# Sending the first four chunks' y to the partitions of their modes through TensorE instead of through transfers

## Chip, cores, metric

One core of a Trainium2 chip. The metric is the device time of one execution in microseconds, taken as the median of repeated runs; the spans in the profile run from the first to the last instruction and are some 2 us shorter.

## The reference, cut to what matters

```python
attn_out = softmax(causal(q @ k.T / 8) + min(bias(s), 0)) @ v        # per batch and head
x  = attn_out -> (8, 576, 512)
X  = rfft(x, axis=1)[:, :64]                                         # 64 modes
Yr = einsum('bmd,mde->bme', Xr, w_r) - einsum('bmd,mde->bme', Xi, w_i)
Yi = einsum('bmd,mde->bme', Xr, w_i) + einsum('bmd,mde->bme', Xi, w_r)
y  = irfft(Y, n=576, axis=1)
u  = x + y
out = u + relu(u @ w_ch)
```

The 64 modes have two weight matrices of 512x512 in fp32 each: 134 MB that pass through the core once. Modes are worked in eight chunks of eight. `y` in the kernel is a chunk's (Yr, Yi) before the inverse transform. Its rows lie on partitions as (mode part, batch); the inverse transform needs a tile `yv` whose partitions are the mode parts alone, with batch in the free dimension, for both `y` and `y @ w_ch`.

## The kernel before

```python
def spread(c, which, rows):                    # one transfer of 128 KB inside SBUF
    nc.sync.dma_start(out=yv[16 * c : 16 * c + 16, :, which, :], in_=rows)

def modes(g, c, meanwhile=None):               # four loads of 512 KB, four column groups
    ps = auxpool.tile([P, DM], FP32, name="yp", tag="aux")
    ...                                        # 16 matmuls; L441
    else:                                      # the last group of channels
        yb = spool.tile([P, DM], FP16, name="y_sb", tag="y")
        ...                                    # yb = ps + y_acc; L455
        spread(c, 0, yb)
        return yb

def first_times_wch(b):                        # y @ w_ch of chunks 0 to 3, one batch; L644, L648
    vp = auxpool.tile([P, DM], FP32, name="v_ps", tag="aux")
    n = 2 * MC * NY                            # 64
    for dt in range(DT):
        nc.tensor.matmul(
            vp[:n], yt_first[:, dt].rearrange("p c (x b) -> p (c x) b", b=B)[:, :, b],
            wch_sb[:, dt, :], start=(dt == 0), stop=(dt == DT - 1),
        )
    nc.vector.tensor_copy(out=yv[:n, b, 1, :], in_=vp[:n])

TAKE = (3, 2, 2, 0, 2, 1)                      # pieces of the x work after each chunk
for c in range(NCK - 2):
    yb = modes(NG - 1, c)
    for x in range(TAKE[c] - 1):
        work()
    yt = y_transposed(yb, c)                   # kept in yt_first for c < NY = 4
    if TAKE[c]:
        work()
    if c >= NY:
        y_times_wch(c, yt)                     # product, copy, spread(c, 1, vb)
    elif c == NY - 1:
        for b in range(B):
            first_times_wch(b)
work()
...                                            # chunks 6 and 7, then 32 output tiles
```

`auxpool` has two PSUM tiles of 128x512 fp32; `upool` has two of 128x512 and `zpool` two of 128x1024. (The expectations call a piece of 128x512 a bank.) So `y @ w_ch` of the first four chunks already goes through kept transposes (a batch's 64 columns are the stationary operand; the trace has weight loads of 128x64 at L644 and copies of 64x512 from `v_ps` to `yv` at L648), while their `y` goes by transfer.

The softmax here doesn't subtract the row's maximum and nothing guards it: scores larger than these inputs give would overflow.

## Time and profile before

| | before |
|---|---|
| median of 3 runs (range) | 459.39 us (458.98 to 459.42) |
| span of the profiled run | 457.1 us |
| DMA engines full | in slices 1 to 36 of 40 |
| last weight load consumed | 418.11 us |
| tail after it | 39.0 us |
| gather after chunk 3, on TensorE | 377.18 to 386.13 us |

The first two rows are results; the others come from the views that the prediction quotes. The kernel is a stream of weight loads with a tail of 39.0 us that the change leaves as it is. In a timeline line the columns are start in us, length in us, engine, source line, operation, output and inputs, shapes and count; brackets give the idle time before it and what ended it. PE is TensorE's matmuls, PEld its weight loads, DVE VectorE, ACT ScalarE, POOL GpSimd, SP SyncE. The clock that is quoted is the share of its full clock that TensorE was granted. The gather is the stage after chunk 3 that brings results of chunks 0 to 3 to the partitions of `yv`; the tail is all that follows the last load; a closed run is a stretch of TensorE work without waits.

### The profile page before, as it was taken

How to read it: one execution, taken by the hardware profiler on the slowest of the kernel's cores; microseconds unless marked ns; L12 is line 12 of the kernel's file. 1: busy time of each engine (PE TensorE's matmuls, PEld its weight loads, DVE VectorE, ACT ScalarE, POOL GpSimd, SP SyncE). 2: the span in 40 equal slices, each digit the busy share in tenths (PEclk: the TensorE clock that was granted, in tenths of full speed). 3: DMA queues.
4: the chain of work that ended last, by engine and by line, in shares of the span. 5: the costliest groups of instructions: out<-in, count | busy, mean ns of one | idle time of the engine just before them, and what ended most of it. 6: DMA issues, size and time to landing. Idle time of an engine off the chain costs nothing.

```text
span 457.1 us, 10262 instructions
## 1 busy us (share of the span) xinstructions
PE 339.1 (74%) x4177; PEld 217.2 (48%) x4209; DVE 237.3 (52%) x528; ACT 219.1 (48%) x382; POOL 182.9 (40%) x269
## 2 busy tenths in 40 slices
PE   1779968966562979936587766779967769797995
PEld 1556646644341656614355544446643326343432
DVE  7777645653242556624345544466656425442675
ACT  1587856554241747723445345446622220221895
POOL 6755555544345555344454444355423223200000
PEclk9999999998586889957778799899999778999999
DMA  9999999999999999999999999999999999995688
GB/s 177 201 203 203 202 201 204 202 204 204 204 204 201 202 202 202 204 205 204 199 192 205 204 204 204 204 203 202 207 206 212 210 210 210 214 214 105 235 285 319
DMA packets 109375, 94.54 MB, mean 207 GB/s; under 512 B 28480, under 2 KB 104512, under 8 KB 109328
## 3 DMA queue, kind: packets, MB, share of 16 engines
q0 software_dynamic: 98960, 81.81, 113.0%
q1 hardware_dynamic: 10368, 12.07, 8.5%
q8 instruction: 33, 0.54, 0.4%
q14 instruction: 14, 0.11, 0.1%
HBM read 164.56 MB, written 9.44 MB: 381 GB/s over the span
## 4 chain that ended last, share of the span: by engine, by line
DMA 70%; PE 20%; issue 4%; POOL 3%; DVE 2%; DVEq 0%; POOLq 0%
DMA w_sb<-in_moe_w_i_dram 44%; DMA q<-in_q_dram 13%; DMA w_sb<-in_moe_w_r_dram 5%; PE yp L441 3%; PE sc_ps L365 3%; PE av_ps L394 2%; DMA x_all<-in_moe_w_r_dram 2%; DMA k<-in_k_dram 2%; PE sc_ps L359 2%; DMA y_acc<-in_moe_w_i_dram 2%; PE tr_ps L324 2%; DMA y_acc<-in_moe_w_r_dram 2%; PE u_ps L694 2%; PE z_ps L675 2%; PE u_ps L675 2%
## 5 line engine op out<-in xcount | busy, mean ns | idle before, releaser
L373 ACT ACTIVATE p_sb<-sc_ps,cumt_sb 128x576 f16<-128x576 f32 (+1 forms) x256 | 141.9, 636 | 45.8 <-PE sc_ps L365 45.4
L217 POOL DMA_DIRECT2D w_sb<-in_moe_w_i_dram x60 | 45.1, 751 | 81.7 <-PE yp L441 36.8
L217 POOL DMA_DIRECT2D w_sb<-in_moe_w_r_dram x60 | 45.4, 757 | 65.2 <-DMA w_sb<-in_moe_w_r_dram 26.1
L217 POOL DMA_DIRECT2D v<-in_v_dram x72 | 50.8, 707 | 31.3 <-DMA w_sb<-in_moe_w_r_dram 8.4
L324 PE MATMUL tr_ps<-ident,q 64*64 64x64 bf16 x576 | 17.1, 208 | 55.4 <-DMA q<-in_q_dram 55.4
L359 PE MATMUL sc_ps<-negm,ident 128*128 128x256 bf16 x256 | 55.0, 300 | 0.3
L441 PE MATMUL yp<-w_sb,xs 128*32 128x512 bf16 x480 | 37.0, 408 | 22.2 <-DMA w_sb<-in_moe_w_i_dram 18.1
L327 DVE COPY qtA<-tr_ps 64x576 bf16<-64x576 bf16 x32 | 23.8, 743 | 50.8 <-PE tr_ps L324 50.7
L344 ACT ACTIVATE p<-sc_ps,cumt 128x64 f16<-128x64 f32 x32 | 10.1, 314 | 74.2 <-PE sc_ps L340 74.2
L394 PE MATMUL av_ps<-v,p_sb 128*128 128x65 f16 x1024 | 43.7, 196 | 0.0
L394 PEld LDWEIGHTS <-p_sb 128*128 128x128 f16 x1024 | 38.9, 99 | 4.8 <-issue 0.7
L327 DVE COPY ktA<-tr_ps 64x576 bf16<-64x576 bf16 x32 | 24.0, 750 | 32.7 <-PE tr_ps L324 32.7
L324 PEld LDWEIGHTS <-q 64*64 64x64 bf16 x576 | 13.3, 120 | 58.0 <-DMA q<-in_q_dram 56.9
L441 PEld LDWEIGHTS <-xs 128*32 128x32 bf16 x512 | 22.9, 169 | 32.3 <-issue 28.8
L365 PE MATMUL sc_ps<-qtB,ktB 128*128 128x64 bf16 (+2 forms) x160 | 34.8, 322 | 3.7 <-issue 2.4
L365 PE MATMUL sc_ps<-qtA,ktA 65*128 65x512 bf16 (+2 forms) x192 | 36.1, 297 | 0.3 <-DVE ktA L327 0.3
L399 DVE TENSOR_REDUCE den<-av_ps 128x5 f32<-128x10 f32 x64 | 10.8, 169 | 46.4 <-PE av_ps L394 46.4
L404 DVE TENSOR_TENSOR x_all<-av_ps,rcp 128x320 f16<-128x320 f32 x64 | 31.5, 492 | 2.2
L327 ACT COPY ktB<-tr_ps 64x576 bf16<-64x576 bf16 x32 | 20.3, 634 | 19.7 <-DVE ktA L327 18.8
L365 PEld LDWEIGHTS <-ktB 128*128 128x128 bf16 x192 | 22.4, 117 | 14.8 <-issue 6.3
L324 PE MATMUL tr_ps<-ident,k 64*64 64x64 bf16 x576 | 17.5, 210 | 14.0 <-DVE qtB L327 10.5
L601 PE MATMUL z_ps<-wch_sb,xs 128*128 128x512 f16 x96 | 26.2, 423 | 0.8 <-DVE xs L595 0.8
(112 smaller groups left out, 526.4 us busy)
## 6 DMA issues: line engine op xcount, KB each, us to landing
w_sb<-in_moe_w_r_dram POOLq DMA_DIRECT2D x60, 512.0 KB, 11.9
w_sb<-in_moe_w_i_dram POOLq DMA_DIRECT2D x60, 512.0 KB, 11.9
q<-in_q_dram POOLq DMA_DIRECT2D x32, 144.0 KB, 9.7
k<-in_k_dram POOLq DMA_DIRECT2D x32, 144.0 KB, 10.1
v<-in_v_dram POOLq DMA_DIRECT2D x72, 64.0 KB, 9.7
out_dram<-r_sb SPq DMA_DIRECT2D x16, 256.0 KB, 2.3
out_dram<-r_w SPq DMA_DIRECT2D x16, 256.0 KB, 2.6
x_all<-in_moe_w_i_dram POOLq DMA_DIRECT2D x3, 512.0 KB, 10.0
```

The source lines that it names most:

```text
L217: nc.gpsimd.dma_start(out=dst, in_=src)
L324: nc.tensor.transpose(ps[rows, r, :], src[rows, r, :], ident16[rows, rows])
L327: copy(out=dst[n % NQ][rows, :].rearrange("d (p r) -> d p r", r=R), in_=ps[rows].rearrange("d r p -> d p r"),)
L359: nc.tensor.matmul(ps[:, bass.ds(w * S, W)], ident16, negm[:, bass.ts(r, W)], start=True, stop=False, skip_group_check=True,)
L365: nc.tensor.matmul(ps[:, c0 : c0 + i1 - i0], keys[:, w, r, :], qt[:, i0:i1], start=False, stop=True, skip_group_check=True,)
L373: nc.scalar.activation(out=pt[:, poff[x] : poff[x] + S - w * W], in_=ps[:, w * S : (w + 1) * S - w * W], func=ACTF.Exp, bias=cumt_sb[:, x, ...
L394: nc.tensor.matmul(ps[:, I, r : r + NCH], lhsT, rhs, start=(i == 0), stop=(i == len(todo) - 1), skip_group_check=True,)
L399: nc.vector.tensor_reduce(out=den, in_=ps[:, :, 0 : VW : NCH], axis=mybir.AxisListType.X, op=ALU.add)
L404: nc.vector.tensor_tensor(out=x_all[:, g, b, :, D * h : D * h + D], in0=ps[:, :, 1 : NCH], in1=rcp.unsqueeze(2).to_broadcast([P, NT, D]), ...
L441: nc.tensor.matmul(ps[32 * cg : 32 * cg + 32, :], cols[:, c0 : c0 + 32, c * MC + 2 * cg + par], wt[(g, c, ri, par)][:, cg, :], start=(x == ...
L601: nc.tensor.matmul(z[:, x, :], xts[i][:, x, dt, :], wch_sb[:, dt, :], start=(dt == 0), stop=(last and dt == DT - 1), skip_group_check=True,)
L675: nc.tensor.matmul(dst[x][r, :], G_sb[rows, bass.ds(T * P, r.stop - r.start)], yv[rows, bb, which, :], start=start, stop=True, skip_group_ ...
```

## The change

Intent: take four transfers out of the full stretch of the DMA engines, and have TensorE, which has waits (1.94, 1.17 and 0.68 us for loads after this stage), do their work: the identity as moving operand selects a batch's `y` just as `w_ch` gives its product. The outputs are 64 partitions tall, so two batches go side by side in two column groups, and the copies out of PSUM alternate between ScalarE and VectorE.

```diff
--- before.py
+++ after.py
@@ -455,7 +455,8 @@
                 nc.vector.tensor_tensor(
                     out=yb[:, cols], in0=ps[:, cols], in1=y_acc[:, c, cols], op=ALU.add
                 )
-            spread(c, 0, yb)
+            if c >= NCK // 2:
+                spread(c, 0, yb)
             return yb
 
     halves = [slice(i * DM // 2, (i + 1) * DM // 2) for i in range(2)]
@@ -637,15 +638,31 @@
         spread(c, 1, vb)
         return vb
 
-    def first_times_wch(b):
-        vp = auxpool.tile([P, DM], FP32, name="v_ps", tag="aux")
-        n = 2 * MC * NY
-        for dt in range(DT):
-            nc.tensor.matmul(
-                vp[:n], yt_first[:, dt].rearrange("p c (x b) -> p (c x) b", b=B)[:, :, b],
-                wch_sb[:, dt, :], start=(dt == 0), stop=(dt == DT - 1),
-            )
-        nc.vector.tensor_copy(out=yv[:n, b, 1, :], in_=vp[:n])
+    def gather(c0, c1):
+
+        n = 2 * MC * (c1 - c0)
+        rows = slice(2 * MC * c0, 2 * MC * c1)
+        ng = P // n
+        for b0 in range(0, B, ng):
+            vp = auxpool.tile([P, DM], FP32, name="v_ps", tag="aux")
+            yp = auxpool.tile([P, DM], FP32, name="yg_ps", tag="aux")
+            for which, ps in ((1, vp), (0, yp)):
+                for dt in range(DT):
+                    for g in range(ng):
+                        op = yt_first[:, dt, : c1 - c0].rearrange("p c (x b) -> p (c x) b", b=B)
+                        nc.tensor.matmul(
+                            ps[n * g : n * g + n, :] if which else ps[n * g : n * g + n, bass.ts(dt, P)],
+                            op[:, :, b0 + g],
+                            wch_sb[:, dt, :] if which else ident16h,
+                            start=(dt == 0 or not which), stop=(dt == DT - 1 or not which),
+                            tile_position=(0, n * g), skip_group_check=True,
+                        )
+                for g in range(ng):
+                    dst, src = yv[rows, b0 + g, which, :], ps[n * g : n * g + n, :]
+                    if g % 2:
+                        nc.vector.tensor_copy(out=dst, in_=src)
+                    else:
+                        nc.scalar.copy(out=dst, in_=src)
 
 
     ahead = []
@@ -744,8 +761,7 @@
         if c >= NY:
             y_times_wch(c, yt)
         elif c == NY - 1:
-            for b in range(B):
-                first_times_wch(b)
+            gather(0, NY)
     work()
     assert not order_z and not ahead
     c = NCK - 2
```

## The prediction

> **What bounds the kernel now.** I read the busy table by slices first, then the chain that ended last, then the transfers, then the timeline of the stage that the change touches. The page of the kernel before, busy tenths in 40 equal slices (the last line is the mean of the 16 DMA engines):
>
> ```profile
> PE   1779968966562979936587766779967769797995
> DVE  7777645653242556624345544466656425442675
> ACT  1587856554241747723445345446622220221895
> DMA  9999999999999999999999999999999999995688
> ```
>
> No compute engine is full before the last slices; DMA is full in the first 36 of 40. The chain that ended last, 370 to 424 us (start, length, what):
>
> ```profile
> 374.94 20.59 DMA w_sb<-in_moe_w_i_dram
> ...
> 396.06 22.01 DMA w_sb<-in_moe_w_i_dram
> 418.07 0.04 issue
> 418.11 0.48 PE yp L441 x4
> ```
>
> So the kernel is a stream of weight loads that ends at 418.07 us, and a tail of 39 us (457.1 - 418.1) that starts with the mode product of the last load. In the tail nothing is touched by the change. The time can move in two ways only: the last load lands earlier or later, or TensorE is not ready for it.
>
> Is the stream limited by the engines' rate or by when loads are issued? The loads of 360 to 420 us show, as the minimum, median and maximum from issue to landing:
>
> ```profile
> DMA to landing us min/median/max: 19.7/20.8/22.0
> ```
>
> A load is 512 KB as written. What the software queue moved in 364 to 369 us (no spread in flight) and in 375 to 381 us (one spread in flight), from the transfers view (packets, MB, share):
>
> ```profile
> q0 software_dynamic: 1024, 1.02, 122.9%
> ```
> ```profile
> q0 software_dynamic: 1155, 1.15, 114.9%
> q1 hardware_dynamic: 142, 0.13, 8.2%
> ```
>
> 1.02 MB in 5 us is 0.204 MB per us, so a load takes 0.524/0.204 = 2.6 us of service, and 20.8 us to landing means that some eight loads stand in the queue. A late issue of one or two us therefore costs nothing; bytes taken out of the engines' work do count. The last load is issued at 396.06, 22 us ahead of its landing.
>
> [...]while the spread of 0.13 MB is in flight, the weights' queue moves 1.15 MB in 6 us where 6 x 0.204 = 1.22 would have gone. [...]before, the eight evacuations of this stage are all on VectorE, 683 ns each. [...]a weight load of 64 columns from the kept transposes is 192 ns at least, one of 128 columns is 97 or 98 ns. [...]the granted clock is 0.53 in 375.9 to 380.9 us, after a stretch with 1.32 us of TensorE work in 5, and 1.00 in 381 to 386.
>
> **The change, part by part.**
>
> Removed: four spreads of y, 128 KB each, at chunks 0 to 3 (issued between 343 and 376 us, so all inside the full stretch). What is one worth? By the two windows above it pushes out 1.22 - 1.15 = 0.07 MB of weights, 0.36 us. Over a longer stretch, 340 to 410 us, the same view has
>
> ```profile
> q0 software_dynamic: 13754, 13.66, 117.3%
> q1 hardware_dynamic: 1184, 1.08, 5.9%
> ```
>
> At 0.204 MB per us, 70 us would hold 14.3 MB of weights; 13.66 went, so 1.08 MB of the hardware queue pushed out some 0.62 MB, 0.57 to 0.6 of its size. It is less than one for one[...]. A spread of 0.131 MB thus costs 0.075 to 0.08 MB / 0.204 = 0.37 to 0.39 us. A count of packets in two-microsecond bins from 300 to 412 us gives 0.43. I take 0.40; four are 1.6 us. The four spreads of later chunks, and those of their products, stay.
>
> Replaced: the stage after chunk 3, in the groups of 374 to 394 us (busy us, mean ns, then idle before):
>
> ```profile
> L644 PE MATMUL v_ps<-wch_sb,yt_first 128*64 128x512 f16 x32 | 9.0, 441 | 0.7 <-ACT yt_first L626 0.7
> L644 PEld LDWEIGHTS <-yt_first 128*64 128x64 f16 x32 | 6.3, 199 | 3.3 <-issue 1.6 <-ACT yt_first L626 0.9
> L648 DVE CAST yv<-v_ps 64x512 f16<-64x512 f32 x8 | 5.5, 683 | 5.6 <-PE v_ps L644 5.6
> ```
>
> Its 32 matmuls run one after another: 0.427 us apart at half clock, 0.213 at full, from 377.18 to 386.1. After the change the same 32 run in two column groups, so in pairs: 16 x 0.213 = 3.4 us at full clock. That such groups overlap is seen in the mode products: 16 of 128x512 in four groups take 1.12 us together, not 16 x 0.213. Added are 32 matmuls against the identity, 128 columns each; estimated at 0.05 us each from the 8 transposes of 64x128 in 0.39 us: 1.6 us. Evacuations: 16, of 64x512, eight each on VectorE (8 x 0.683 = 5.5, as before) and on ScalarE (some 0.6 each from its 128x512 copy of 592 ns, so 4.8 us, where it is nearly idle: 0.59 us busy in 376.5 to 386.5).
>
> With two PSUM buffers, a round (products, then identity) goes: 0.85 us of products, 0.1 to the copies, 0.68 of copies, 0.1 back, then the buffer is free: about 1.7 us a round, and 0.85 + 0.4 of TensorE work fits inside. Four rounds without the last copies are 3 x 1.7 + 1.3 = 6.4 us, plus about 1.3 us for the half clock of the first round: 7.7 us against 8.9 before. If weight loads of 192 ns do not overlap at all, 64 of them are 12.3 us, 3.4 us longer than now.
>
> Does TensorE then arrive late? The timeline has its waits after this stage:
>
> ```profile
> 395.57 0.46 PE L441 MATMUL yp<-w_sb,xs 128*32 128x512 bf16 x4 [1.94 <-DMA w_sb<-in_moe_w_i_dram]
> ...
> 415.13 0.46 PE L441 MATMUL yp<-w_sb,xs 128*32 128x512 bf16 x4 [1.17 <-DMA w_sb<-in_moe_w_i_dram]
> ...
> 418.11 0.45 PE L441 MATMUL yp<-w_sb,xs 128*32 128x512 bf16 x4 [0.68 <-DMA w_sb<-in_moe_w_i_dram]
> ```
>
> It waits 1.94 us for chunk 5's last load, then has a nearly closed run of work to 413.9, then waits 1.17 and 0.68. The whole of this moves with the loads. Only a stage that ends over 1.9 - 1.6 = 0.3 us later than now would eat into it, and the next 1.85 us of waits (1.17 + 0.68) would take up most of even the 3.4 us case. So TensorE's side is worth 0 in the sum. Sum: 459.39 - 1.6 = **457.8 us**, 0.35% faster.
>
> **Rivals.** (a) The gather becomes the bound: weight loads don't overlap between the two groups, or the copies hold the two buffers. For it: 192 ns a load, 64 of them. Against: mode products overlap loads of 131 to 216 ns four deep. Its worst, 12.3 us, leaves the time at about 458 to 459.5. (b) One byte for one byte: the spreads cost as much as weights. 4 x 0.131/0.204 = 2.6 us, 456.8. Against: the two counts of displaced bytes. (c) The spreads were hidden: the DMA engines had gaps that they filled. Then 459.4. Against: the share stays above 1.2 throughout and the weights' rate dips each time. (d) The clock: [...]a half-clock window in the tail would cost up to 3.4/2 = 1.7 us. Against: counted from the matmul records, no stretch of 3.4 us between 401 us and the last matmuls is less than 0.63 busy, while the windows after which a full clock was halved were under 0.5.
>
> **Range and chances.** (b) sets the low end and (a) or (c) the high: 456.9 to 458.8. A 2% move is 9.2 us, six times the sum, and neither rival comes near: faster 0.01, same 0.98, slower 0.01.
>
> **What would show it.** Right: four spreads gone from the hardware queue; the last weight load lands about 416.5 instead of 418.07; the tail is still 39.0 us; the stage after chunk 3 takes 7 to 9 us of TensorE; ScalarE has eight more copies of about 0.6 us there; the wait of chunk 5 for its load is at least 1 us. Wrong: a landing at 418 in spite of the missing spreads (c), TensorE arriving at the last load without a wait (a), or a tail longer than 39.3 us with a granted clock below 0.98 (d).

The sum is 459.39 - 4 x 0.40 = 457.8 us. The 0.40 us rests on the counts of displaced bytes. The steps of 0.1 us in a round are estimates; the trace of before has 0.04 us from a matmul's end to the copy that waits for it (376.51 to 376.55) and from that copy's end to the next matmul (377.14 to 377.18). The 1.3 us for the half clock is an estimate too, about what the 0.85 + 0.4 us of one round lose at half clock. The 3.4 us of rival (d) is the length of the shortest whole half-clock stretches in the trace of before (3.41 us, for instance from 397.68); that such a stretch in the tail would cost half its length is the author's estimate, from the 0.427 us of a matmul at half clock against 0.213 at full.

## The result, and the profile after

| | before | after |
|---|---|---|
| median of 6 runs each | 459.19 us | 458.26 us |
| range | 458.7 to 459.65 | 457.09 to 459.76 |
| ratio (95% interval) | | 0.9981 (0.9961 to 1.0001) |

A ratio here is the mean time of one kernel's fast runs over that of the other's in the same rounds, so it isn't quite the ratio of the medians quoted beside it. Measured twice more, the changed kernel gave 0.9962 (0.9944 to 0.9979) and 0.9966 (0.9952 to 0.9979): it is some 0.2 to 0.4% faster, 0.9 to 1.75 us. In the first six its runs scatter more than those of before (standard deviation 0.95 against 0.35 us).

The profiled run of the changed kernel was the slowest of its six (459.76 us). Its span, 458.0 us, is longer than before's 457.1, so spans alone would mislead here. Its stream of loads was late already before the change begins: counted from the transfer records of the queue that carries the weights (earlier loads of q, k and v included, in bytes as written), 68 MB had come by 345.47 us, against 344.50 in the trace before. Stretches must be compared, not end points.

**The stream.** The transfers view over 340 to 410 us of the changed kernel, as the prediction showed it for before (13.66 and 1.08 MB there):

```profile
q0 software_dynamic: 14188, 14.09, 121.5%
q1 hardware_dynamic: 464, 0.43, 2.4%
```

In the same 70 us the weights' queue moved 0.43 MB more, for 0.65 MB less on the other queue: 0.66 for one. The transfer records give it more sharply. From 68 to 76 MB of that queue, which is the stretch in which the four spreads ran, the kernel before took 385.26 - 344.50 = 40.76 us and the changed one 384.51 - 345.47 = 39.04: **1.72 us, 0.43 per spread**. All twelve traces told of here agree: 40.8 us in the two with these spreads (before and e2), 39.0 to 39.1 in the ten without.

**The gather.** The groups of 374 to 392 us in the changed kernel (busy us, mean ns, idle before and its releasers); the prediction showed the same view of before:

```profile
L653 PE MATMUL v_ps<-wch_sb,yt_first 128*64 128x512 f16 x32 | 7.9, 638 | 3.5 <-DVE yv L663 2.9 <-ACT yt_first L627 0.7
L653 PE MATMUL yg_ps<-ident16h,yt_first 128*64 128x128 f16 x32 | 2.9, 315 | 0.0
L663 DVE CAST yv<-v_ps 64x512 f16<-64x512 f32 x4 | 2.8, 692 | 10.2 <-ACT yv L665 10.2
L665 ACT CAST yv<-v_ps 64x512 f16<-64x512 f32 x4 | 2.3, 579 | 9.0 <-PE v_ps L653 9.0
```

TensorE waits for VectorE's copies (2.9 us), and VectorE's copies wait not for TensorE but for ScalarE's (10.2 us). One round in the timeline shows the order:

```profile
384.15 1.98 PE L653 MATMUL v_ps<-wch_sb,yt_first 128*64 128x512 f16 x8 [0.95 <-DVE yv L663]
...
385.82 0.77 PE L653 MATMUL yg_ps<-ident16h,yt_first 128*64 128x128 f16 x8
386.17 0.58 ACT L665 CAST yv<-v_ps 64x512 f16<-64x512 f32 x1 [2.32 <-PE v_ps L653]
...
386.79 0.69 DVE L663 CAST yv<-v_ps 64x512 f16<-64x512 f32 x1 [2.08 <-ACT yv L665]
...
387.53 1.98 PE L653 MATMUL v_ps<-wch_sb,yt_first 128*64 128x512 f16 x8 [0.95 <-DVE yv L663]
```

A round is 384.15 to 387.53, 3.38 us: 1.67 of products at half clock (until the identity's begin, 385.82 - 384.15), 0.35 to the first copy, the two copies one after the other, and the buffer is free. Four rounds are 377.39 to 390.91: **13.5 us, against 9.0 before**. The windows of the gather and of the tail (length, busy us and instructions of PE, PEld, DVE, ACT and POOL, then granted clock, DMA share, GB/s):

```profile
377.30:390.90 13.60, 9.70 (x64) 7.38 (x65) 4.63 (x8) 4.28 (x9) 2.22 (x3) 0.50 1.24 206
419.40:458.00 38.60, 33.33 (x171) 14.39 (x170) 24.53 (x40) 27.74 (x31) 0.00 (x0) 1.00 0.71 252
```

The clock is at half (0.50) through the whole gather. And the mode product of the last load, which before came after a wait of 0.68 us, now has none:

```profile
419.44 0.47 PE L441 MATMUL yp<-w_sb,xs 128*32 128x512 bf16 x4
```

So TensorE, not the stream, sets when the tail begins in this run: the last packet of the weights had landed 2.1 us earlier, at 417.32 us (before: 417.74, 0.4 us earlier). The page says the same in its chain that ended last, for before and for the changed kernel (two pages, one line each):

```profile
DMA 70%; PE 20%; issue 4%; POOL 3%; DVE 2%; DVEq 0%; POOLq 0%
```
```profile
DMA 53%; PE 32%; DVE 6%; issue 4%; POOL 3%; ACT 1%; DVEq 0%; POOLq 0%
```

The theory to test: the four spreads cost the stream 1.7 us and that is the gain; the slow gather, slow because two engines' copies stand in line and because the clock stays at half (0.50), gives part of it back.

### The profile page after: what moved, and what is told of

Same layout as the page of the kernel before. It is cut to its first block, busy times and chain, and to the rows that moved or that the text cites. A ratio compares the mean times of both kernels' runs of the same rounds, so it can differ in the third digit from the quotient of the medians.

```text
span 458.0 us, 10354 instructions
## 1 busy us (share of the span) xinstructions
PE 349.1 (76%) x4241; PEld 220.4 (48%) x4241; DVE 236.5 (52%) x528; ACT 223.5 (49%) x390; POOL 182.6 (40%) x269
## 4 chain that ended last, share of the span: by engine, by line
DMA 53%; PE 32%; DVE 6%; issue 4%; POOL 3%; ACT 1%; DVEq 0%; POOLq 0%
DMA w_sb<-in_moe_w_i_dram 28%; DMA q<-in_q_dram 13%; DMA w_sb<-in_moe_w_r_dram 5%; PE sc_ps L365 4%; DMA x_all<-in_moe_w_i_dram 4%; PE av_ps L394 4%; PE yp L441 3%; PE sc_ps L359 3%; PE tr_ps L324 2%; DMA y_acc<-in_moe_w_r_dram 2%; PE z_ps L602 2%; DMA k<-in_k_dram 2%; PE z_ps L692 2%; PE ft_ps L418 2%; PE u_ps L711 2%
## 5 line engine op out<-in xcount | busy, mean ns | idle before, releaser
L324 PE MATMUL tr_ps<-ident,q 64*64 64x64 bf16 x576 | 18.1, 215 | 52.9 <-DMA q<-in_q_dram 52.8
L359 PE MATMUL sc_ps<-negm,ident 128*128 128x256 bf16 x256 | 57.1, 310 | 0.2
L365 PE MATMUL sc_ps<-qtB,ktB 128*128 128x512 bf16 (+2 forms) x192 | 45.2, 354 | 0.0
L365 PE MATMUL sc_ps<-qtA,ktA 65*128 65x512 bf16 (+2 forms) x192 | 37.4, 305 | 0.6 <-DMA qtA<-ncum_sb 0.6
L602 PE MATMUL z_ps<-wch_sb,xs 128*128 128x512 f16 x96 | 27.4, 437 | 0.8 <-DVE xs L596 0.8
```

Of the source, the lines that this page charges most:

```text
L324: nc.tensor.transpose(ps[rows, r, :], src[rows, r, :], ident16[rows, rows])
L359: nc.tensor.matmul(ps[:, bass.ds(w * S, W)], ident16, negm[:, bass.ts(r, W)], start=True, stop=False, skip_group_check=True,)
L365: nc.tensor.matmul(ps[:, c0 : c0 + i1 - i0], keys[:, w, r, :], qt[:, i0:i1], start=False, stop=True, skip_group_check=True,)
L602: nc.tensor.matmul(z[:, x, :], xts[i][:, x, dt, :], wch_sb[:, dt, :], start=(dt == 0), stop=(last and dt == DT - 1), skip_group_check=True,)
```

## The experiments

| run | what differs | median us | ratio to before (95%) |
|---|---|---|---|
| e1_no_spread | before, four spreads left out | 457.68 | 0.9957 (0.9942 to 0.9973) |
| e2_keep_spread | changed, four spreads kept as well | 459.23 | 0.9996 (0.998 to 1.0012) |
| e3_wide, e9_wide_again | gather with more PSUM | 457.19, 456.89 | 0.9953 (0.9936 to 0.9969), 0.9952 (0.994 to 0.9964) |
| e4_after_again, e10_after_third | the changed kernel | 457.5, 457.92 | 0.9962 (0.9944 to 0.9979), 0.9966 (0.9952 to 0.9979) |
| e5_dve_only | copies on VectorE alone | 458.83 | 0.9986 (0.9963 to 1.0009) |
| e6_filler | added matmuls in the gather | 457.69 | 0.997 (0.9946 to 0.9994) |
| e7_wide_take | wide, x work moved | 457.03 | 0.9952 (0.9929 to 0.9975) |
| e8_wide_take6 | as e7, chunks 4 and 5 too | 460.38 | 1.0017 (0.9995 to 1.0039) |

Runs e1 to e4 shared a chip and its runs of before (median 459.28), e5 to e8 the next (459.09), e9 and e10 a third (459.0).

### e1_no_spread: the transfers' part alone

```diff
-            spread(c, 0, yb)
+            if c >= NCK // 2:
+                spread(c, 0, yb)
...
+    nc.vector.memset(yv[: 2 * MC * (NCK // 2), :, 0, :].bitcast(FP32), 0.0)
```

> Kernel before without the four early spreads (their rows are zeroed once by VectorE, so the result is wrong on purpose). Nothing else is changed: the transfers' part of the change alone. Theory (the spreads took 0.4 to 0.55 us of the weight stream each, and TensorE gave part of that back in the changed kernel): 1.6 to 2.2 us faster than before, about 457.3; chunk 5 and the last load still waited for by TensorE. Rival 1 (the spreads were worth no more than the changed kernel gained): about 0.9 us faster. Rival 2 (hidden): no change.

Measured: 0.9957, which is 1.97 us off 459.3. The stretch from 68 to 76 MB took 39.04 us, the same as in the changed kernel. TensorE waits for the last load as it did before (timeline):

```profile
414.59 0.45 PE L441 MATMUL yp<-w_sb,xs 128*32 128x512 bf16 x4 [1.17 <-DMA w_sb<-in_moe_w_i_dram]
...
417.52 0.46 PE L441 MATMUL yp<-w_sb,xs 128*32 128x512 bf16 x4 [0.64 <-DMA w_sb<-in_moe_w_i_dram]
```

The spreads weren't hidden, and by the times their removal is worth what the stream gains (1.97 us, interval 1.2 to 2.7, against 1.72). The end of this one trace shows less of it: counted from the 68 MB mark the last packet lands only 0.7 us earlier than before (72.6 against 73.2 us), because the last 0.8 MB took 7.5 us instead of 6.4. In the twelve traces this last piece takes 5.9 to 7.5 us, and the DMA engines are no longer full there (share 0.62 in 413.9 to 418.1 us of before); what sets it was not tested. (The result passed the comparison with the reference although these rows of `y` were zero: `y` is small in this problem, and the comparison doesn't see it. "Correct" says little about the gather here, in any of these runs.)

### e2_keep_spread: TensorE's part alone

```diff
-            if c >= NCK // 2:
-                spread(c, 0, yb)
+            spread(c if c >= NCK // 2 else c + NCK // 2, 0, yb)
```

> Changed kernel that also keeps the four spreads (into rows that later spreads overwrite, so the result stays right): the TensorE part of the change alone. Theory (the gather takes 13.6 us instead of 9 and TensorE becomes the bound of the last chunks): slower than the changed kernel by 1.2 to 1.6 us as the gather starts later, so 0.3 to 1.5 us slower than before; no wait of TensorE for the last load. Rival (the gather is off the path): the same as before within 0.2 us.

Measured: 0.9996. The theory's direction (up to 1.5 us slower than before) wasn't seen in the time; the rival's number was, but not for the rival's reason. TensorE is on the path in this trace: the last load's product starts at 420.41 us without a wait, 1.7 us after the last packet (418.72), and the run is the slowest of its six (460.99 us, 1.8 above their median). That in the other runs the gather's extra 4.5 us just fit into the waits that the kernel before had (1.94, 1.17 and 0.68 us at the loads of the late chunks, and about 0.8 for chunk 5's sum) is argued, not shown. Against the changed kernel of the same rounds this run is 0.9996/0.9962, 0.34% or 1.6 us, slower (1.9 us by the plain means). So the spreads are worth 1.6 to 1.9 us with the gather and 1.97 without.

### e3_wide: more PSUM for the gather

```diff
-            vp = auxpool.tile([P, DM], FP32, name="v_ps", tag="aux")
-            yp = auxpool.tile([P, DM], FP32, name="yg_ps", tag="aux")
-            for which, ps in ((1, vp), (0, yp)):
+            if b0 // ng % 2 == 0:
+                vps = [auxpool.tile([P, DM], FP32, name="v_ps", tag="aux") for g in range(ng)]
+                yps = [upool.tile([P, DM], FP32, name="yg_ps", tag="u") for g in range(ng)]
+            else:
+                vps, yps = (
+                    [t[:, g, :] for g in range(ng)]
+                    for t in (zpool.tile([P, 2, DM], FP32, name="z_ps", tag="z") for i in range(2))
+                )
+            for which, pss in ((1, vps), (0, yps)):     # group g in pss[g]
```

> Changed kernel with the gather's two column groups each in a PSUM bank of its own, and eight banks in turn instead of two, so that the copies of ScalarE and VectorE can run side by side and TensorE need not wait for them. Theory: the gather takes 6 to 8 us instead of 13.6, TensorE waits for the last load again, and the time falls to that of the run without spreads (about 457.3, 1.6 to 2.2 us faster than before). Rival (the gather's length is not what limits): the same as the changed kernel, 458.3.

Measured: 0.9953. The gather runs from 375.21 to 382.04 us, 6.8 us, and the clock comes back within it (mean 0.75, where the changed kernel had 0.50). In the rounds where each column group has a tile of its own the copies run side by side (376.92 and 376.96 us); where the two groups have the halves of one tile, VectorE still waits for ScalarE, 1.45 us (timeline):

```profile
376.92 0.58 ACT L671 CAST yv<-v_ps 64x512 f16<-64x512 f32 x1 [1.76 <-PE v_ps L659]
376.96 0.69 DVE L669 CAST yv<-v_ps 64x512 f16<-64x512 f32 x1 [2.88 <-PE v_ps L659]
...
379.70 1.30 DVE L669 CAST yv<-z_ps 64x512 f16<-64x512 f32 x2 [1.45 <-ACT yv L671]
```

The wait is in the program: among the semaphores that the built kernels wait on, all eight VectorE copies of the changed kernel wait on ScalarE; in the wide one the four from tiles of their own wait on TensorE, the four from shared tiles on ScalarE. It follows the tile, even where the two groups have different halves of it. No run here tried such copies without the order, so whether the memory needs it was not tested.

The last load's product has no wait in this trace (416.04 us), so TensorE was still a little late in this run. In e9, a second profile of the same kernel, it waits 0.71 us. The time equals that of e1 without spreads.

### e4_after_again and e10_after_third: the changed kernel again

> The changed kernel again, beside the others on the same chip: 0.5 to 1.5 us faster than before. Theory: the gather takes 13 to 14 us at half clock and TensorE reaches the last load without a wait in this trace too. If a trace shows a gather under 10 us, the half clock was chance.

> The changed kernel a third time, beside the wide version. Theory: 0.2 to 0.35% faster than before, with half clock through the whole gather of 13.5 us and no wait of TensorE for the last load. Rival: as the wide version, 0.4 to 0.5% faster.

Measured: 0.9962 and 0.9966. The gather took 375.01 to 388.52 and 376.31 to 389.82 us, 13.5 us both times, and the last load's product had no wait in either, so the slow gather isn't chance.

### e9_wide_again: is the gather's length worth anything?

> The wide version again, beside the changed kernel on one chip, because their intervals against the kernel before overlap so far (0.9953 against 0.9962 and 0.9981). Theory (the slow gather gives back part of what the missing spreads win): 0.4 to 0.5% faster than before, and faster than the changed kernel of the same rounds by 0.1 to 0.25%. Rival (the gather's length is worth nothing): the two within 0.05%.

Measured: 0.9952. In the rounds that they share, the changed kernel's mean is 1.0009 and 1.0016 times the wide one's. Over both, 12 runs against 11, the difference is 0.55 us with a standard error of 0.25 (from the scatter of the runs). So the slow gather gives back about half a microsecond, which these runs fix only to within 0.05 to 1.05. The traces point the same way: TensorE begins the last load's product 2.13, 0.77 and 1.44 us after the last packet in the three traces of the changed kernel, 0.65 and 0.50 in those of the wide one, and 0.36 in the one of before.

### e5_dve_only: one engine for the copies

```diff
-                    if g % 2:
-                        nc.vector.tensor_copy(out=dst, in_=src)
-                    else:
-                        nc.scalar.copy(out=dst, in_=src)
+                    nc.vector.tensor_copy(out=dst, in_=src)
```

> Changed kernel with all sixteen copies of the gather on VectorE. Theory (a copy by VectorE of one column group starts only when ScalarE's of the other group in the same PSUM bank is done, so two engines buy nothing): the gather takes 13.5 us as in the changed kernel, give or take 0.5, with half clock; the time is within 0.3 us of the changed kernel's, 1 to 2 us faster than before. Rival (the two engines share the work): eight more copies of 0.69 us make the gather 3 to 5 us longer, TensorE later by as much, and the time 2 us or more above the changed kernel's.

Measured: 0.9986. The gather took 375.54 to 389.10 us, 13.6 us with sixteen copies on one engine where two engines had 13.5. A round in the timeline:

```profile
384.20 1.39 DVE L662 CAST yv<-v_ps 64x512 f16<-64x512 f32 x2 [0.65 <-PE v_ps L653]
...
385.64 1.98 PE L653 MATMUL v_ps<-wch_sb,yt_first 128*64 128x512 f16 x8 [1.03 <-DVE yv L662]
```

The theory held for the stage: in the changed kernel the second engine buys nothing (13.5 us against 13.6). That it is a matter of the bank, as the theory has it, was not shown; by e3 it is the tile. (It began at full clock for half a microsecond, so its first round was 3.17 us; the later ones are 3.46, against 3.38 with two engines.) The time, expected within 0.3 us of the changed kernel's, was 0.2 us above it by the first of the changed kernel's ratios and 1.1 by the second; the intervals overlap, and it isn't settled whether that is more than scatter.

### e6_filler: more work, more clock

```diff
+        fill = zpool.tile([P, 2, DM], FP32, name="z_ps", tag="z")
...
+                if not which:
+                    for f in range(4):
+                        nc.tensor.matmul(
+                            fill[:, f % 2, :], ident16h, wch_sb[:, f, :], start=True, stop=True,
+                            skip_group_check=True,
+                        )
```

> Changed kernel with four more matmuls of 128x512 in each round of the gather, into a bank that nobody reads (work of 0.85 us at full clock, 1.7 at half, in the 0.95 us in which TensorE waits for copies). Theory (the half clock comes from the waits in every round): the clock goes to full after the first one or two rounds and the gather takes 10 to 12 us, less than the 13.5 without the added work; time as the changed kernel or up to 1 us faster. Rival (the half clock belongs to column groups): the clock stays at half, the gather takes 16 us or more and the time rises by 1 us or more.

Measured: 0.997. The gather took 377.83 to 389.29 us, 11.5 us: **two microseconds less with sixteen matmuls more**. The windows view of it:

```profile
377.80:389.30 11.50, 11.42 (x83) 7.24 (x84) 4.65 (x8) 4.24 (x8) 2.23 (x3) 0.85 1.24 206
```

TensorE is busy 11.42 of 11.50 us and its mean clock is 0.85, where the changed kernel had 9.70 of 13.60 and 0.50. So the half clock isn't a property of column groups: with 0.08 us idle in place of 3.90, the same groups got 0.85. In the traces of before and of the changed kernel each whole stretch at one granted clock lasts 3.41 us or a whole multiple of it (up to 18 times, 61.44 us), so the records can be counted in windows of that length. By the matmul records, those inside the changed kernel's gather are 0.71 or 0.72 busy in all its three traces and each is followed by another at half clock.

Over all twelve traces the clock came back from half to full 185 times, never after a window less than 0.80 busy; it fell from full to half 197 times, never after a window more than 0.65 busy. A window 0.72 busy lies between. In the traces of before and of the changed kernel all 35 windows 0.65 to 0.80 busy were followed by another at the clock they had, 26 at full and 9 at half. The gather begins at half clock (in the changed kernel's trace from 375.84 us, the gather from 377.39) or reaches it within half a microsecond (e5), after TensorE's wait for chunk 3's last load (2.05 us in the changed kernel's trace, 2.13 in that of before). (Busy shares here are modelled from matmul records, and some busier windows, 27, stayed at half.)

With the clock at full, a round takes 2.54 us (timeline):

```profile
381.68 1.14 PE L654 MATMUL v_ps<-wch_sb,yt_first 128*64 128x512 f16 x8
...
384.22 1.14 PE L654 MATMUL v_ps<-wch_sb,yt_first 128*64 128x512 f16 x8
```

In time the filler gained nothing that shows: 0.997 on its chip, against 0.9962 and 0.9966 of the changed kernel on two others. So e6 explains the clock, not the time; what the gather's length costs rests on e9.

### e7_wide_take: TensorE's waits used better

```diff
-    TAKE = (3, 2, 2, 0, 2, 1)
+    TAKE = (3, 2, 2, 0, 3, 0)                  # on top of the wide gather
```

> The wide gather (banks of its own for each group) and one piece of the x work moved from after chunk 5 to before it, where TensorE waits for loads (1.5 and 2.0 us in the trace of the wide version). Theory (with the wide gather TensorE is still late at the last load by about 0.6 us): the last load is waited for again and the time falls by 0.3 to 0.8 us against the wide version, to 2.3 to 3 us faster than before. Rival (the loads' end is the bound already): as the wide version, 2.0 to 2.2 us faster than before.

Measured: 0.9952, no better than the wide one; the rival was right. TensorE waits for three of the last five loads again (1.20, 1.64 and 0.41 us in the timeline). With the loads waited for again and no time gained, the wide version's gain is about all that these four spreads give.

### e8_wide_take6: four more transfers out

```diff
-            if c >= NCK // 2:
+            if c >= NCK - 2:
                 spread(c, 0, yb)
...
-        if c >= NY:
-            y_times_wch(c, yt)
-        elif c == NY - 1:
+        if c == NY - 1:
             gather(0, NY)
+        elif c == NCK - 3:
+            gather(NY, NCK - 2)                # four groups of 32 partitions
```

> As the run before it, and chunks 4 and 5 go through a second gather too (four column groups of 32, two rounds), so that four more transfers (two spreads of y, two of y@w_ch) are gone. Theory (a transfer of 128 KB takes 0.5 us of the weight stream): the loads end another 1.5 to 2 us earlier; TensorE has about 1.3 us more to do in its closed run, so the time falls by 0.5 to 1.5 us more, to 3 to 4 us faster than before, with TensorE reaching the last load without a wait. Rival (TensorE's run to the end is the bound): slower than the run before it by about 1 us.

Measured: 1.0017, slower than e7 by 0.65% or 3 us; the theory fell, and the rival was too mild. The stream did what was expected: 81 MB of the weights' queue had come by 407.77 us, 1.98 us ahead of e7's 409.75 (0.15 of it from before the spreads). But chunks 4 and 5 lie in TensorE's closed run. After the second gather the next x product waits for PSUM that sixteen copies have to leave first (timeline):

```profile
402.05 1.41 DVE L669 CAST yv<-z_ps 32x512 f16<-32x512 f32 x2 [0.64 <-ACT yv L671]
402.80 2.74 PE L602 MATMUL z_ps<-wch_sb,xs 128*128 128x512 f16 x8 [2.53 <-DVE yv L669]
...
418.22 0.47 PE L441 MATMUL yp<-w_sb,xs 128*32 128x512 bf16 x4
```

Two half-clock windows lie about here (mean clock 0.73 from 396.2 to 408.7 us, where TensorE is busy 9.55 of 12.5 us), and the last load is not waited for at 418.22, 1.3 us later than in e7 (416.90), though its last packet had landed 4.5 us before, at 413.71 (e7: 416.51). The tail is also longer, 40.1 us against 38.5. Its first product with all rows of `yv` starts 7.45 us after the last load's, against 6.66 in e7, after a wait of 0.60 us for the last spread, which is 0.8 of the 1.6; the rest was not traced. The same trade that paid for chunks 0 to 3 loses here.

## Why the prediction was right or wrong

- **The stream is the bound up to the last load:** right for before, but for its last 0.8 MB, where the engines are not full (e1). In e1, where nothing but the zeroing is added, less traffic gave less time.
- **0.40 us a spread, 1.6 in sum:** 0.43 and 1.72 in the records of the stream; 1.97 (1.2 to 2.7) in time by e1. Slightly low. The count by packets in bins, 0.43, which I had and rounded down, was the better one. One byte for one (rival b) would have been 2.6; hidden (rival c) would have been 0; the records show neither, though e1's interval alone would not exclude 2.6. That a spread's byte costs less than a weight's also shows in the two views of before: per MB, its queue took 0.64 of the engine time of the weights' queue (5.9%/1.08 against 117.3%/13.66). Why it does was not tested.
- **The gather takes 7.7 us:** wrong; 13.5 us in three traces. The step that failed is "0.85 us of products, 0.1 to the copies, 0.68 of copies, 0.1 back ... about 1.7 us a round", on two counts. The copies of one buffer are not 0.68 us side by side but 0.58 + 0.69 in line, since the program orders two engines on one tile (e3, e5). And the half clock was put at 1.3 us for the first round alone, but it stayed for all of them (0.50), with windows 0.72 busy, and came back when e6 filled the waits (0.85): a round is 3.38 us. The rounds of e6 that ran at full clock, with the same copies, take 2.54 us, so each of the two is worth about half of the 1.7 us by which a round is longer than estimated. The first is visible before a run, in the wait list of the built kernel. The second could be suspected from the estimate itself, which had TensorE idle a quarter of each round and began at half clock: in the trace of before, a half-clock window 0.70 busy (from 117.8 us) was followed by another at half.
- **Rival (a) and the signs of being wrong:** two of the signs that the prediction had set went against it. TensorE arrived at the last load without a wait, and chunk 5's load was not waited for either (400.04 us). Rival (a) came true in its second form, "the copies hold the two buffers". That the sum came out does not make this part right.
- **"If weight loads of 192 ns do not overlap at all":** not the cause. In e3 a group of eight products at full clock takes 379.28 to 380.20, 0.92 us, where eight loads of 192 ns one after another would be 1.54, so the loads of the two column groups overlap. Nor is 192 ns a matter of column groups alone: in the trace of before, loads of 64 columns of `G_sb`, whose matmuls are placed in column groups, take 106 to 110 ns. Why those of the kept transposes take longer was not tested.
- **"TensorE's side is worth 0 in the sum":** nearly. With the spreads in place the longer gather costs nothing measurable (e2). Without them it gives back 0.55 us, give or take 0.25 (e4 and e10 against e3 and e9). The prediction's bound for a gather 3.4 us too long, that the waits take up most of it, came out.
- **Rival (d), the clock in the tail:** not seen; the tail ran at 1.00 and was 38.6 us (before: 0.98 and 39.0). The clock mattered in the gather instead. How many half-clock windows follow the gather differs between traces of the changed kernel (chunk 4's product to chunk 5's took 9.1 us in the first trace and 8.1 in e4's), and its runs scatter by 0.82 us (standard deviation of 18) against 0.52 for the wide version (11); those of before scatter by 0.35 to 0.97, depending on the chip. Whether the one causes the other was not tested.
- **The sum, 457.8 us:** the first six runs gave 458.26, the later ones 457.5 and 457.92. The gain was a little larger than predicted and about half a microsecond of it was given back, so the total is close partly by luck: two errors of opposite sign.

## What to carry to other kernels

Where one stage was full (here the DMA engines, share 1.24), moving work off it paid what that stage's own records show (1.72 us of the stream), and the receiving engine must be checked for where its waits are: the same move paid in a stretch with waits (0.9953 in e3) and lost in a closed run 15 us later (1.0017 in e8). Splitting copies over two engines bought nothing with both column groups in one tile (13.5 us against 13.6 with one engine, e5); with a tile for each in every other round, and more buffers, the gather took 6.8 us (e3). Look at the waits of the built program. This gather began at half clock, left TensorE idle over a quarter of the time and stayed at half throughout, 13.5 us; with sixteen matmuls more in it the clock came back and it took 11.5 (e6).

The best version here is the wide one (e3, e9), 0.9952 to 0.9953 of before; e7 is no different.
